# Six buffers for q and k instead of five, three for x instead of four, and spanning units scored in pairs

## The chip, the cores and the metric

The kernel runs on one core of a Trainium2 chip. The metric is the device time of one execution in microseconds (us), taken as the median of several runs. A profiled execution of the kernel gives the views that are read below.

The core has five engines that run their own instruction streams and wait for each other by semaphores. TensorE (PE in the profile, PEld for its weight loads) does matmuls. VectorE (DVE) does the search for the largest scores. ScalarE (ACT) does copies out of PSUM, exponentials and sines. GpSimd (POOL) does the folding, the splitting into halves and part of the feed-forward arithmetic. SyncE (SP) issues most of the DMAs, in order.

## The reference

Two blocks follow each other. First, attention that keeps only the 32 largest scores of each row, for 8 batches, 8 heads, 576 positions and 64 dimensions a head:

```
scores = scale * q @ k^T                       # (8, 8, 576, 576), scale = 1/8
kth    = 32nd largest of each row
scores = where(scores >= kth, scores, -1e9)
attn   = exp(scores - rowmax) / (rowsum + 1e-9)
x      = attn @ v                              # brought to (4608, 512)
```

Then a feed-forward block on the 4608 rows of x, with w_in of 512 x 2048 and w_out of 2048 x 512, in which the hidden value h is gated by its own cosine:

```
h   = x @ w_in
out = (h * cos(h)) @ w_out
```

## The kernel before

**Units and slots.** The 8 x 576 = 4608 tokens are cut into 36 tiles of 128 tokens. Each tile and each pair of heads (hp, 0 to 3) makes one unit, 144 in all, numbered 4 x tile + hp. The loop runs over 144 slots. In slot i VectorE searches the largest scores of unit i, ScalarE masks and exponentiates unit i-1, GpSimd splits unit i-2 into 16-bit halves, and SyncE writes these to DRAM (`rows`, L407) and reads them back transposed (`pT`, L413). In every even slot TensorE multiplies units i-4 and i-3 with v (`values`, L434), and VectorE scales the result into `xT` (L442).

**Spanning units.** A batch has 576 = 4.5 x 128 tokens. So the tile in the middle of each two batches holds 64 tokens of one batch and 64 of the next: tiles 4, 13, 22 and 31, units 16 to 19, 52 to 55, 88 to 91 and 124 to 127. Such a unit has two `parts` and needs q and k of both batches. In what follows 4t is the number of the first of the four units.

**Scoring.** `scores` (L226) makes the scores of a unit: columns 0 to 447 go into a PSUM tile `sc`, of which there are two, columns 448 to 575 into one of two ends of the PSUM tile `rim`, whose rest (`room`) takes the result of `values`. ScalarE copies both to SBUF in `take_scores` (L236, L237), and VectorE reads `sc` once more in `fold_high` (L245). A table `scored` says in which slot a unit is scored. A unit is scored one slot ahead (i - 1), but an even unit two slots ahead (i - 2), together with the odd unit before it: so two units are scored in an even slot and none in an odd one. Spanning units of hp 2 are an exception: `two` is false for them. Of these four units, 4t is scored in slot 4t-2 (with unit 4t-1), 4t+1 alone in slot 4t, 4t+2 alone in slot 4t+1, and 4t+3 with 4t+4 in slot 4t+2. In the profile a matmul in full precision appears as two records; a plain unit has four `sc` records and four `rim` records, a spanning one eight and eight.

**Loads.** `load_qk(b, hp)` brings q and k of a batch and a pair of heads with four DMAs on SyncE (L191 to L194), `load_v` brings v with three (L202, L207). Both take their tiles from the pool `loads`, which has five buffers for q and k each, and six for v. A load is put into the slot in which its buffer's former pair is scored for the last time (`last`), or the next slot that has no load yet (`load_at`). In the slot it comes after the slot's `rows` and `pT` on SyncE's queue.

**Feed-forward.** When the four units of a token tile are done, its feed-forward runs in pieces on TensorE between the attention's matmuls: `ff1` (L491) multiplies with w_in, ScalarE writes each piece twice, to a tile `g` (L505) and a tile `x` (L507), GpSimd reduces the argument (L527, L536), ScalarE takes the sine (L546), GpSimd multiplies `g` by it (L553), and `ff2` (L566) multiplies with w_out. `feed(n)` issues up to n pieces, on a credit that each slot adds to: 5.0, less 0.9 for each unit scored in the slot. In the last slots and after them (`ff["end"]`) VectorE takes GpSimd's part.

**Weights.** At the start the weights come in 32 chunks and are decoded by ScalarE (L133, L136), VectorE (L144) and GpSimd (L154). They are staged in the tiles of `g` (seven, `CHUNKS`) and, for every other one of the first chunks, in those of `x` (`XB`, four). The DMAs of chunks 0 to 9 are on SyncE's queue, the later ones on ScalarE's (L120).

**Order.** The order of the instructions on each engine is the one in which the program writes them down; nothing rearranges them.

Of the kernel before, what the change touches and what calls it, by code (L numbers as in the profile page):

```python
# [10 lines left out]
F32 = mybir.dt.float32  # L11
# [6 lines left out]
P = 128  # L18
# [12 lines left out]
def kernel(  # L31
# [13 lines left out]
    NT = S // P  # L45
# [7 lines left out]
    assert SCALE == 2.0 ** round(math.log2(SCALE)) and TOPK == 32 and HS <= 512  # L53

    consts = ctx.enter_context(tc.tile_pool(name="consts", bufs=1))
    loads = ctx.enter_context(tc.tile_pool(name="loads", bufs=5))
    work = ctx.enter_context(tc.tile_pool(name="work", bufs=2))
    small = ctx.enter_context(tc.tile_pool(name="small", bufs=4))
    ps = ctx.enter_context(tc.tile_pool(name="ps", bufs=2, space=bass.MemoryType.PSUM))
# [30 lines left out]
    for f in range(NF):  # L90
        w = consts.tile([P, DM], F32, tag=f"w_out{f}", name=f"w_out{f}")
        w_out.append(w)
        chunks.append((moe_w_out[f * P : (f + 1) * P, :], w))
    CHUNKS, XB = 7, 4
    BUSY = range(7, 12)
    ff = {"live": 0, "tick": 0, "now": 0, "credit": 0.0, "end": False, "kind": 0, "half": 0, "open": 0, "late": False}

# [64 lines left out]
    for t0 in range(0, B * S, P):  # L162
        parts = []
# [11 lines left out]
    for i in range(2 * NP):  # L175
        t = consts.tile([P, P], F32, tag=f"v_tail{i}", name=f"v_tail{i}")
# [21 lines left out]
    def load_v(b, hp):  # L198
        st = pairs.setdefault((b, hp), {})
        cols = slice(hp * P, (hp + 1) * P)  # L200
        t = loads.tile([P, NT, P], F32, tag="v", name="v", bufs=6)
        nc.sync.dma_start(out=t, in_=v[b, 0:MAIN, cols].rearrange("(c p) e -> p c e", p=P))  # L202
        st["v"] = t

        t = st["v_tail"] = v_tails[b % 2 * NP + hp]
        for j in range(2):
            nc.sync.dma_start(  # L207
                out=t[j * TAIL : (j + 1) * TAIL, j * D : (j + 1) * D],
                in_=v[b, MAIN:S, hp * P + j * D : hp * P + (j + 1) * D],
            )  # L210
# [64 lines left out]
    for i in range(3):  # L275
        t = consts.tile([P, 2, 2], F32, tag=f"dens{i}", name=f"dens{i}")
# [4 lines left out]
    for i in range(3):  # L281
        t = consts.tile([P, 2, TOPK + 1, 2], F32, tag=f"top{i}", name=f"top{i}")
# [345 lines left out]

    scored, last, last_values = {}, {}, {}
    for i, u in enumerate(units):  # L630
        two = i % 2 == 0 and 2 < i and (len(u["parts"]) == 1 or u["hp"] == 0)
        scored.setdefault(i - 2 if two else i - 1, []).append(u)
        for part in u["parts"]:
            last[part[0], u["hp"]] = i - 2 if two else i - 1
            last_values[part[0], u["hp"]] = i
    at_slot, at_once = {}, {}

    def load_at(i, *what):
        while i in at_slot:
            i += 1  # L640
        at_slot[i] = what

    order = [(b, hp) for b in range(B) for hp in range(NP)]
    for n in range(NP, len(order)):
        i = last[order[n - 5]] if n >= 5 else 0
        load_at(max(i, 2 * NP + 2), load_qk, *order[n])
        i = last_values[order[n - 6]] if n >= 6 else 0
        load_at(max(i + 4 - i % 2, 2 * NP + 2), load_v, *order[n])

    for hp in range(NP):  # L650
        at_once[hp] = [(load_v, 0, hp)]
# [110 lines left out]
    for i in range(NU):  # L762
# [3 lines left out]
        u, w, x = (units[i - n] if n <= i else None for n in range(3))  # L766
# [46 lines left out]
```

## Time and profile before

| | |
|---|---|
| median of three runs | 1452.13 us (1447.84 to 1453.05) |
| profiled execution | 1448.69 us, its span 1446.9 us |
| mean granted TensorE clock | 0.975 |
| busy: PE, DVE, POOL, ACT | 95%, 94%, 81%, 75% of the span |
| two ordinary slots | 18.69 us |
| DMA issue to landing, median: q, k, k, k (small) | 3.8, 3.6, 3.7, 3.3 us |

The profile's span is the time from the first to the last instruction. A line of a group names the source line, the engine, the operation, what is written and read, the count, the busy time with the mean of one, and the idle time of the engine ahead of it with what ended it. A line in order of time gives the start, the duration, the engine, the line, the operation and how many records were merged; in brackets it has the idle time of the engine ahead of it and who ended it.

### The profile page before, as it was taken

The numbers are of one execution on the slowest core, as the hardware profiler recorded it, in microseconds if no ns is written. First come the engines' busy times: TensorE is split into PE (matmuls) and PEld (weight loads), VectorE is DVE, ScalarE is ACT, GpSimd is POOL, SyncE is SP. The second block draws the span as 40 slices with busy tenths as digits, with TensorE's granted clock in tenths as the row PEclk, the third lists the DMA queues.
The fourth block names the chain that finished last, engine by engine and source line by source line (L and its number), as shares of the span: only waits on it lengthen the run. The fifth ranks groups of instructions, "written<-read, shape, count | busy, mean of one in ns | idle before, by whom it ended". The sixth has DMA issues, their size and how long they took to land.

```text
span 1446.9 us, 30176 instructions
## 1 busy us (share of the span) xinstructions
PE 1380.3 (95%) x10252; PEld 992.2 (69%) x10252; DVE 1359.4 (94%) x5237; ACT 1082.6 (75%) x1894; POOL 1166.0 (81%) x816
## 2 busy tenths in 40 slices
PE   4388899999999999999999999999999999999998
PEld 2175667777777767777777777777777776777775
DVE  7999999999999999999999999999999999999931
ACT  5787767877777777777777777777877777777742
POOL 5867888888888887888888887888888888888820
PEclk6589999999999999999999999999999999999999
DMA  8987677656665575657765566656666566655540
GB/s 257 287 230 199 175 184 180 160 158 196 174 166 140 160 190 170 170 150 187 183 166 153 145 177 177 177 151 160 197 186 150 140 170 186 156 150 153 149 104 15
DMA packets 438380, 245.25 MB, mean 170 GB/s; under 512 B 386384, under 2 KB 403025, under 8 KB 438225
## 3 DMA queue, kind: packets, MB, share of 16 engines
q1 hardware_dynamic: 429648, 222.13, 58.3%
q10 hardware_dynamic: 8576, 21.19, 4.5%
q8 instruction: 81, 1.33, 0.4%
q14 instruction: 75, 0.61, 0.1%
HBM read 45.09 MB, written 103.81 MB: 103 GB/s over the span
## 4 chain that ended last, share of the span: by engine, by line
PE 87%; DVE 7%; ACT 3%; DMA 2%; SPq 1%; POOL 0%; issue 0%; ACTq 0%
PE mm L491 33%; PE o L566 33%; PE rim L434 11%; PE sc L226 8%; DVE top L337 3%; PE rim L226 2%; DVE rest L342 2%; DMA v<-in_v_dram 1%; DMA st<-in_moe_w_in_dram 1%; DVE rest L245 1%; ACT s L366 0%; ACT s L374 0%; DVE low L342 0%; DVE w_out L144 0%; DMA k<-in_k_dram 0%
## 5 line engine op out<-in xcount | busy, mean ns | idle before, releaser
L491 PEld LDWEIGHTS mm<-xT,w_in 128*128 128x128 f32 x4608 | 536.9, 192 | 75.9 <-issue 65.2
L491 PE MATMUL mm<-xT,w_in 128*128 128x128 f32 x4608 | 539.2, 275 | 7.6 <-ACT x L507 4.8
L566 PE MATMUL o<-w_out,g 128*128 128x512 f32 x1152 | 539.7, 602 | 6.3 <-POOL w_out L154 3.7
L337 DVE MAX8 top<-rest 128x8 f32<-128x288 f32 x1152 | 478.9, 451 | 0.0
L397 POOL COPY halves<-s 128x2304 uint16<-128x2304 uint16 x144 | 303.2, 2105 | 156.4 <-ACT s L374 153.3
L342 DVE MATCH_REPLACE8 rest<-top,rest 128x288 f32<-128x288 f32 x864 | 376.5, 443 | 0.0
L566 PEld LDWEIGHTS o<-w_out,g 128*128 128x128 f32 x1152 | 202.8, 191 | 193.9 <-issue 185.3
L337 DVE MAX8 top<-low 128x8 f32<-128x288 f32 x576 | 243.6, 449 | 0.1
L374 ACT ACTIVATE s<-s,nd 128x576 f32<-128x576 f32 x288 | 220.3, 767 | 0.8
L366 ACT ACTIVATE s<-s,top 128x576 f32<-128x576 f32 x288 | 206.1, 765 | 0.0
L270 POOL TENSOR_TENSOR low<-low,rest 128x576 int32<-128x576 int32 x139 | 196.5, 1414 | 10.9
L261 POOL TENSOR_TENSOR low<-s 128x576 int32<-128x576 int32 x139 | 196.4, 1413 | 4.4 <-ACT s L237 4.4
L226 PE MATMUL sc<-k,q 64*128 64x448 f32 (+1 forms) x640 | 155.5, 587 | 37.3 <-DMA k<-in_k_dram 15.6
L505 ACT ACTIVATE g<-mm 128x512 f32<-128x512 f32 x144 | 85.9, 596 | 134.5 <-PE mm L491 130.4
L536 POOL TENSOR_TENSOR x<-g,x 128x1024 f32<-128x1024 f32 x68 | 161.0, 2367 | 5.7
L434 PE MATMUL rim<-pT,v 128*64 128x128 f32 (+1 forms) x2560 | 159.7, 269 | 5.3 <-DMA pT<-rows 5.3
L553 POOL TENSOR_TENSOR g<-g,x 128x1024 f32<-128x1024 f32 x68 | 161.0, 2368 | 0.0
L434 PEld LDWEIGHTS rim<-pT,v 128*64 128x64 f32 x2560 | 133.1, 139 | 16.1 <-issue 4.3
L236 ACT COPY s<-sc 128x896 f32<-128x896 f32 x144 | 129.3, 898 | 3.4 <-PE sc L226 2.9
L342 DVE MATCH_REPLACE8 low<-top,low 128x288 f32<-128x288 f32 x288 | 125.4, 444 | 0.0
L237 ACT COPY s<-rim 128x256 f32<-128x256 f32 x144 | 55.1, 383 | 91.8 <-PE rim L434 91.8
L226 PEld LDWEIGHTS sc<-k,q 64*128 64x128 f32 (+1 forms) x640 | 47.2, 182 | 99.9 <-DVE rest L342 47.0
(47 smaller groups left out, 1307.4 us busy)
## 6 DMA issues: line engine op xcount, KB each, us to landing
rows<-halves SPq DMA_DIRECT2D x144, 640.0 KB, 3.0
out_dram<-ob ACTq DMA_DIRECT2D x36, 256.0 KB, 2.3
q<-in_q_dram SPq DMA_DIRECT2D x31, 288.0 KB, 3.8
v<-in_v_dram SPq DMA_DIRECT2D x32, 256.0 KB, 3.5
st<-in_moe_w_out_dram ACTq DMA_DIRECT2D x16, 512.0 KB, 6.0
st<-in_moe_w_in_dram SPq DMA_DIRECT2D x10, 512.0 KB, 6.9
k<-in_k_dram SPq DMA_DIRECT2D x31, 144.0 KB, 3.6
k<-in_k_dram SPq DMA_DIRECT2D x32, 128.0 KB, 3.7
```

What stands on the lines that cost most here:

```text
L226: nc.tensor.matmul(to[r0 : r0 + rows, j, 0 : k1 - k0], st["q"][d, q0 : q0 + rows], st["k"][d, k0:k1], start=True, stop=True,)
L261: nc.gpsimd.tensor_tensor(out=u["low"].bitcast(I32), in0=s[:, :, 0:HS], in1=s[:, :, HS:S], op=ALU.add)
L270: nc.gpsimd.tensor_tensor(out=low, in0=low, in1=u["rest"][:, :, HS:S].bitcast(I32), op=ALU.subtract)
L337: nc.vector.max(to[:, j], src[:, j])
L342: nc.vector.match_replace(rest[:, j], to[:, j], src[:, j], NEG)
L366: nc.scalar.activation(out=s[:, j], in_=s[:, j], func=AF.Prelu, bias=less[:, j, 1:2], scale=1.0, alpha=FAR)
L374: nc.scalar.activation(out=s[:, j], in_=s[:, j], func=AF.Exp, bias=nd[:, j : j + 1], scale=SCALE, accum_out=den[:, j, 0:1],)
L397: nc.gpsimd.tensor_copy(out=halves[:, :, 0 : 2 * S], in_=s.rearrange("p (k h) -> p h k", h=2))
L434: nc.tensor.matmul(o[d, to], lhsT, rhs, start=c == 0, stop=c == NT)
L491: nc.tensor.matmul(mm[:, at : at + w], w_in[f // FC][:, c, (f % FC) * P : (f % FC + 1) * P], blk["xT"][:, c], start=c == 0, stop=c == NC - 1,)
L536: nc.gpsimd.tensor_tensor(out=x, in0=g, in1=x, op=ALU.subtract)
L566: nc.tensor.matmul(o, g[:, at : at + P], w_out[f], start=f == 0, stop=f == NF - 1)
```

## The change

Three things change. The pool of q and k has six buffers (v keeps six), and a load is put into the slot of the last scoring of the pair six before it instead of five. The tile `x` has three buffers instead of four, which also sets how many weight chunks are staged there. And `two` holds for every even unit after the second, so that in each of the four places unit 4t+2 is scored in slot 4t together with 4t+1, and slot 4t+1 scores nothing. A q and a k buffer together are 4,608 bytes in each partition, an x buffer 4,096.

```diff
-    loads = ctx.enter_context(tc.tile_pool(name="loads", bufs=5))
+    loads = ctx.enter_context(tc.tile_pool(name="loads", bufs=6))
...
-    CHUNKS, XB = 7, 4
+    CHUNKS, XB = 7, 3
...
-        t = loads.tile([P, NT, P], F32, tag="v", name="v", bufs=6)
+        t = loads.tile([P, NT, P], F32, tag="v", name="v")
...
-        two = i % 2 == 0 and 2 < i and (len(u["parts"]) == 1 or u["hp"] == 0)
+        two = i % 2 == 0 and 2 < i
         scored.setdefault(i - 2 if two else i - 1, []).append(u)
...
     for n in range(NP, len(order)):
-        i = last[order[n - 5]] if n >= 5 else 0
+        i = last[order[n - 6]] if n >= 6 else 0
         load_at(max(i, 2 * NP + 2), load_qk, *order[n])
```

## The prediction

> **What bounds the kernel now.** I read the page first for the busy shares and the chain of work that ended last, then the busy time by stretch, then the order of time on TensorE, then the waits.
>
> ```profile
> span 1446.9 us, 30176 instructions
> ...
> PE 1380.3 (95%) x10252; PEld 992.2 (69%) x10252; DVE 1359.4 (94%) x5237; ACT 1082.6 (75%) x1894; POOL 1166.0 (81%) x816
> ...
> PE 87%; DVE 7%; ACT 3%; DMA 2%; SPq 1%; POOL 0%; issue 0%; ACTq 0%
> ```
>
> The chain is TensorE for 87% of the span, VectorE for 7%. Next come stretches that run from the first values matmul (L434) of an even slot to that of a later one. The columns are length, then busy time and instruction count of PE, PEld, DVE, ACT and POOL, then clock, DMA share and GB/s.
>
> ```profile
> 426.05:463.43 37.38, 37.38 (x274) 27.12 (x272) 36.96 (x146) 29.28 (x52) 32.22 (x23) 1.00 0.54 149
> 482.13:500.98 18.85, 18.85 (x147) 13.47 (x145) 18.64 (x75) 15.04 (x28) 16.27 (x12) 1.00 0.54 154
> 159.45:201.43 41.98, 40.72 (x300) 27.69 (x296) 41.98 (x163) 32.35 (x58) 38.16 (x27) 1.00 0.72 190
> 500.98:539.60 38.62, 38.62 (x301) 26.87 (x297) 38.26 (x150) 29.93 (x54) 34.49 (x24) 1.00 0.70 190
> 839.14:879.02 39.88, 39.46 (x300) 27.61 (x296) 39.51 (x155) 30.27 (x54) 35.75 (x25) 1.00 0.68 184
> 1178.57:1217.04 38.47, 38.47 (x300) 26.94 (x296) 38.10 (x149) 29.78 (x54) 34.37 (x24) 1.00 0.68 190
> ```
>
> The first line is four ordinary slots: 37.38 us, TensorE without a gap, VectorE busy for 36.96. So TensorE sets the pace and VectorE has 0.42 us to spare per four slots. The second line is two slots in which one spanning unit and one plain unit are scored: 18.85 against 18.69, so a spanning unit costs TensorE 0.15 us more. The last four lines are the four places where batches meet inside a token tile (slots 16 to 19, 52 to 55, 88 to 91, 124 to 127), each as it stands on TensorE's queue. They are 1.1 to 4.6 us longer than ordinary.
>
> Where that time goes shows on TensorE in the third place:
>
> ```profile
> 866.36 1.16 PE L226 MATMUL sc<-k,q 64*64 64x448 f32 x8
> 867.16 0.58 PE L226 MATMUL rim<-k,q 64*64 64x128 f32 x8
> 867.67 1.98 PE L566 MATMUL o<-w_out,g 128*128 128x512 f32 x4
> ...
> 874.87 0.97 PE L226 MATMUL sc<-k,q 64*64 64x448 f32 x4
> 876.26 1.06 PE L226 MATMUL sc<-k,q 64*64 64x448 f32 x3 [0.42 <-DMA k<-in_k_dram]
> 876.77 0.64 PE L226 MATMUL rim<-k,q 64*64 64x128 f32 x6
> 877.16 0.54 PE L226 MATMUL sc<-k,q 64*64 64x448 f32 x1
> 877.54 0.38 PE L226 MATMUL rim<-k,q 64*64 64x128 f32 x2
> 877.85 1.02 PE L226 MATMUL sc<-k,q 64*128 64x448 f32 x4
> ```
>
> One spanning unit takes 1.13 us where nothing holds it (start 1205.78 to the next form at 1206.91). Unit 90 here takes 867.67 - 866.36 = 1.31, unit 91 takes 877.85 - 874.87 = 2.98, broken into pieces. The profile names only 0.42 us of it as idle, because the ends of matmuls are modelled; the rest hides inside stretched matmuls. The loads that these units need leave SyncE's queue just before:
>
> ```profile
> 861.82 0.53 SPq L191 DMA_DIRECT2D q<-in_q_dram  x1
> ...
> 870.85 0.58 SPq L191 DMA_DIRECT2D q<-in_q_dram  x1
> ...
> 872.64 1.00 SPq L194 DMA_DIRECT2D k<-in_k_dram  x1
> ```
>
> The page's DMA issues give 3.3 to 3.8 us from issue to landing. Issued at 870.85 to 873.64, they land near 876.3, and the units at 874.87 wait. VectorE shows the echo: "DVE xT L442 <- ACT s L237" is 7.0 us in 4 waits between 157 and 1371 us, one in each of slots 18, 54, 90 and 126.
>
> **What the Trainium skill says.** "Perfetto Trace Analysis", section "Identifying the Most-Contended Engine", holds matmul busy time a poor measure and names a repeated bubble as a sign of too few buffers. Both agree here: 0.42 us of named idle stands for 2 us lost, and the bubble returns every 36 slots. "DMA: Bandwidth & Descriptors", section "Anatomy of one DMA", says that a wait sits on the issuing sequencer, never in the DMA engine. The trace agrees: the loads of one slot come out only after the transpose ahead of them on SyncE (861.73, then 861.82). "TensorE: Matmul & The Clock Gate", part 1, says that a gap above some 3.4 us halves the clock; the gaps here stay below, and the clock is 1.00 in all six stretches, so no clock is to be won.
>
> **The change, part by part.**
>
> *Six q and k buffers.* Pair n now takes the buffer of pair n-6, so each load from batch 1, pair 1 on takes the slot that its predecessor had. That moves 27 loads of four DMAs. In a meeting place of slots 4t to 4t+3, pair 2 of the new batch leaves in slot 4t-2 instead of 4t, pair 3 in 4t instead of 4t+1. Slots with a load stay the same ones, except that slot 12 gains one (and pushes three v DMAs to slot 13) and slot 125 loses one. SyncE in slot 12 is free from 147.3, after the v load, to 150.0, in slot 13 from 156.1 to 159.0; a q,k load takes 2.3 to 2.9 us of it, the v load 1.8. Cost: 0, hidden by those gaps; without them rows and transpose go up to 1 us later, and the values matmuls that use them come at least a slot after.
>
> *Two at a time.* In each of the four places one spanning unit's eight sc and eight rim records move from slot 4t+1 to slot 4t, ahead of 40 values records (L434), 32 of L491 and 8 of L566. In slot 4t+1 nothing is scored then, so ScalarE copies the next unit's scores (L236, L237, 1.27 us) ahead of the exponentials, as in other odd slots. The order on VectorE and GpSimd is unchanged; TensorE's and ScalarE's only there. The work is equal. Behind the moved scores wait values and feed-forward matmuls of slot 4t; the score waits for the load issued in slot 4t-2 (503.59 to 506.54 in the second place, needed near 518.9) and PSUM that plain even slots free in time too. Pair 3 is issued at 522.42 to 524.74 and needed near 537, over 8 us after landing. So both waits go, and nothing else in the place is late.
>
> *Sum, by stretches.* A place should take 37.38 + 3 x 0.15 = 37.83 us (three of the four units scored in it span; the first spanning unit is scored just ahead of it). The first place also keeps a TensorE wait of 1.43 us for xT at 165.48 (0.11 is the usual distance, 1.54 is seen), so 39.26. Savings: 41.98 - 39.26 = 2.72; 38.62 - 37.83 = 0.79; 39.88 - 37.83 = 2.05; 38.47 - 37.83 = 0.64. Together **6.2 us**. *Sum, by waits*, a second way: time of the late units over 1.13. First place 2.34 and 2.53, so 2.61; second 1.90, 0.77; third 1.31 and 2.98, 2.03; fourth 1.75, 0.62. Together 6.0 us. The two agree, so the lone score itself costs almost nothing; the late load is the whole effect.
>
> *Three x tiles.* An x tile lives 21.1 us (L507 of its first half at 426 to 1300 us, gate L553 ending). Three tiles turn over in 3 x 18.69 = 56.1 us, so 35 us remain; in the tail the least is 28 us. Cost 0. At the start weight chunks 9 and 11 go into g tiles instead of x tiles. Chunk 7 then waits on SyncE for chunk 1's add (L154), which ends by 18.4, and SyncE gets there at 23.7; chunk 14 waits on ScalarE's queue for chunk 6, whose add ends by 40.54, and is issued at 41.96 (its predecessor at 41.59). Cost 0 with a margin of only 1.05 us. If the adds slip, q and k loads of the start and ScalarE's issues behind them slip by the same; bound: -1 to +5 us (one batch of four adds is 5.03). I take 0.
>
> The sum is against the profiled execution, 1448.69 us with a span of 1446.9: 1442.5. It stands 3.4 us below the median of 1452.13, which I carry unchanged: **1445.9 us**, 0.43% faster.
>
> **Rivals.**
> - *The waits are larger without the profile's luck.* They differ by place from 0.62 to 2.61 us, so they depend on when a landing falls. If the 3.4 us between the profiled execution and the median lie there, the gain is 9.6: 1442.5. For: the spread of the runs is 5.2 us. Against: the start has waits for DMA as well, 15.2 us of them in TensorE's view.
> - *VectorE takes the pace.* With 0.42 us to spare per four slots it could hide half of the gain: about 3 us, 1449. Against: its work in a place is 36.95 (slots 16 to 19, 52 to 55 alike), while TensorE needs 37.83.
> - *Slower: a weight chunk holds a queue at the start.* Fewer x tiles mean older tiles to wait for. Should chunk 14 and those behind it miss their add by a whole slot, ScalarE's queue is held for 10 us twice, and VectorE's masks and TensorE's scores with it: 20 - 6 = +14, 1466. It turns the sign once the holds exceed 6 us. Against: every chunk had its add done, the tightest 1.05 us early.
> - *The change does nothing*: a load could still wait on SyncE behind a transpose. Against: two slots, some 19 us, lie between issue and use.
>
> **How the numbers follow.** The forecast and its neighbours between 3 and 8 us saved: 0.6. Larger waits: 0.27. VectorE or nothing gained: 0.07. Slower: 0.06. A measurement of this kernel can tell about 0.5%, 7.3 us, from no change. The forecast lies 1.1 us short of it, so faster gets the 0.27 and 0.19 of the 0.6: 0.46; same the other 0.41 and 0.07: 0.48; slower 0.06. The range runs from 1439.5 (9.6 us gained, and 3 us of the runs' own spread) to 1452.0 (nothing gained).
>
> **What would show it.** Right: each place takes 37.8 us, the first about 39.3; spanning scores in unbroken eights of 1.13 us, two units one after the other in slots 16, 52, 88 and 124; TensorE's wait for k after 157 us gone; the four L442 waits of 7.0 us gone or below 1 us. Wrong: sc still broken at units 18, 19, 54, 55; VectorE gapless and TensorE with gaps in those slots; or waits of L120 and L133 grown before 60 us.

## The result, and the profile after

The changed kernel takes 1440.53 us in the median of six runs (1440.07 to 1444.68); six runs of the kernel before, three of which stand in the table above, give 1452.59 us. The ratio is 0.993, with a 95% interval of 0.9907 to 0.9952: faster by 0.7%. The profiled execution took 1440.07 us, the fastest of the six, where that of before took 1448.69.

The page of the changed kernel opens as follows; the last line is the chain by engine.

```profile
span 1438.3 us, 30154 instructions
...
PE 1372.0 (95%) x10252; PEld 989.1 (69%) x10252; DVE 1359.6 (95%) x5237; ACT 1082.4 (75%) x1894; POOL 1164.8 (81%) x816
...
PE 89%; DVE 5%; ACT 2%; DMA 2%; SPq 0%; POOL 0%; issue 0%; ACTq 0%
```

TensorE is busy for 8.3 us less (1380.3 before), with the same 10252 records, and the span is 8.6 us shorter. VectorE's busy time is unchanged (1359.4). So nearly all of what went away lay inside matmuls that the profile had counted as busy.

The busy time by stretch of the changed kernel follows, over the four places where batches meet, with the same ends on TensorE's queue as in the prediction, from the first values matmul of slot 4t-2 to that of slot 4t+2 (length; then busy and count for PE, PEld, DVE, ACT, POOL; clock; DMA share; GB/s):

```profile
158.28:197.34 39.06, 37.76 (x300) 26.85 (x296) 39.05 (x152) 31.26 (x56) 34.25 (x24) 1.00 0.74 192
496.89:534.38 37.49, 37.49 (x300) 26.77 (x296) 36.96 (x145) 29.27 (x53) 32.19 (x23) 1.00 0.69 196
833.93:871.42 37.49, 37.49 (x300) 26.77 (x297) 36.95 (x145) 29.26 (x53) 32.20 (x23) 1.00 0.69 195
1170.96:1208.46 37.50, 37.50 (x300) 26.78 (x297) 36.98 (x145) 29.27 (x53) 32.20 (x23) 1.00 0.66 179
```

Before, these were 41.98, 38.62, 39.88 and 38.47 us. The differences are 2.92, 1.13, 2.39 and 0.97: **7.4 us**. The other 1.2 us of the span lie ahead of the first place: its first line starts at 158.28 instead of 159.45. Between the places nothing moved.

Inside the third place, TensorE in order of time (start, duration, line, records):

```profile
850.47 0.98 PE L226 MATMUL sc<-k,q 64*64 64x448 f32 x8
851.27 0.40 PE L226 MATMUL rim<-k,q 64*64 64x128 f32 x8
851.49 0.93 PE L226 MATMUL sc<-k,q 64*64 64x448 f32 x8
852.24 0.40 PE L226 MATMUL rim<-k,q 64*64 64x128 f32 x8
852.57 1.09 PE L434 MATMUL rim<-pT,v 128*64 128x128 f32 x16
...
860.30 3.60 PE L566 MATMUL o<-w_out,g 128*128 128x512 f32 x8
863.73 3.73 PE L491 MATMUL mm<-xT,w_in 128*128 128x128 f32 x32
...
869.12 0.98 PE L226 MATMUL sc<-k,q 64*64 64x448 f32 x8
869.92 0.40 PE L226 MATMUL rim<-k,q 64*64 64x128 f32 x8
870.25 1.02 PE L226 MATMUL sc<-k,q 64*128 64x448 f32 x4
```

Units 89 and 90 stand one behind the other, 2.10 us for both (850.47 to 852.57), and unit 91 takes 1.13 us (869.12 to 870.25). All three are unbroken. The load that unit 91 needs now leaves on SyncE at 855.70 to 858.03:

```profile
855.70 0.53 SPq L191 DMA_DIRECT2D q<-in_q_dram  x1
...
857.44 0.59 SPq L194 DMA_DIRECT2D k<-in_k_dram  x1
```

It is issued 13.4 us ahead of the unit's first matmul, where before these were 4.0 us (870.85 to 874.87).

Every wait of VectorE between 157 and 1371 us in the changed kernel (who waited for whom; total, times, longest):

```profile
DVE den L382 <- ACT s L374: 14.6, 60, 0.4
```

Before, the same question gave two lines:

```profile
DVE den L382 <- ACT s L374: 15.1, 59, 0.4
DVE xT L442 <- ACT s L237: 7.0, 4, 2.5
```

The four waits of L442 are gone. On TensorE the wait for k is gone too, and one wait of 1.3 us for xT is left, in the first place.

### The profile page after: what moved, and what is told of

The parts are those of the page before. It is cut to its first block, busy times and chain, and to the rows that moved or that the text cites. A ratio compares the mean times of both kernels' runs of the same rounds, so it can differ in the third digit from the quotient of the medians.

```text
span 1438.3 us, 30154 instructions
## 1 busy us (share of the span) xinstructions
PE 1372.0 (95%) x10252; PEld 989.1 (69%) x10252; DVE 1359.6 (95%) x5237; ACT 1082.4 (75%) x1894; POOL 1164.8 (81%) x816
## 4 chain that ended last, share of the span: by engine, by line
PE 89%; DVE 5%; ACT 2%; DMA 2%; SPq 0%; POOL 0%; issue 0%; ACTq 0%
PE mm L491 34%; PE o L566 34%; PE rim L434 11%; PE sc L226 8%; DVE top L337 2%; PE rim L226 2%; DVE rest L342 1%; DMA st<-in_moe_w_in_dram 1%; DMA v<-in_v_dram 0%; ACT s L366 0%; DVE rest L245 0%; ACT s L374 0%; DVE low L342 0%; DVE w_out L144 0%; ACT x L507 0%
## 5 line engine op out<-in xcount | busy, mean ns | idle before, releaser
L491 PEld LDWEIGHTS mm<-xT,w_in 128*128 128x128 f32 x4608 | 536.9, 192 | 75.0 <-issue 65.2
L566 PE MATMUL o<-w_out,g 128*128 128x512 f32 x1152 | 537.1, 600 | 10.0 <-POOL w_out L154 7.7
L491 PE MATMUL mm<-xT,w_in 128*128 128x128 f32 x4608 | 539.2, 275 | 6.7 <-ACT x L507 4.8
L566 PEld LDWEIGHTS o<-w_out,g 128*128 128x128 f32 x1152 | 202.7, 190 | 197.6 <-issue 185.3
L226 PE MATMUL sc<-k,q 64*128 64x448 f32 (+1 forms) x640 | 151.4, 591 | 35.7 <-DVE rest L245 13.5
L245 DVE TENSOR_TENSOR rest<-sc,s 128x576 f32<-128x576 f32 x144 | 107.7, 748 | 6.5 <-ACT s L237 6.5
```

The costliest lines, as they stand in the source:

```text
L226: nc.tensor.matmul(to[r0 : r0 + rows, j, 0 : k1 - k0], st["q"][d, q0 : q0 + rows], st["k"][d, k0:k1], start=True, stop=True,)
L491: nc.tensor.matmul(mm[:, at : at + w], w_in[f // FC][:, c, (f % FC) * P : (f % FC + 1) * P], blk["xT"][:, c], start=c == 0, stop=c == NC - 1,)
L566: nc.tensor.matmul(o, g[:, at : at + P], w_out[f], start=f == 0, stop=f == NF - 1)
```

## The experiments

Three explanations stood against each other: the late loads, which six buffers move ahead; the order on TensorE, which scoring in pairs changes; and the start, where three x tiles could help or hurt. No run has the pairs with five buffers, or six buffers with four x tiles. Every kernel was timed beside the kernel before on the same chip. In the first group that gave 54 runs of before with a median of 1449.97 us (1447.6 to 1461.4). The six runs that gave 1452.59 thus lie somewhat high for this kernel.

### Three x tiles alone

```diff
-    CHUNKS, XB = 7, 4
+    CHUNKS, XB = 7, 3
```

> The kernel before with three x tiles and nothing else. If the x tiles cost nothing (the prediction) and the shorter start of the changed kernel's profile (1.2 us) is chance: the four places stay at 38.5 to 40 us (the first near 42), time within 2 us of before, ratio 1.000. Rival, the x tiles shorten the start: about 1.2 us faster and slots 0 to 3 some 1 us shorter. Rival, the start stalls: slower by up to 5 us.

Measured: 1449.49 us, ratio 0.9989 (0.9974 to 1.0004). The places by stretch:

```profile
158.51:201.11 42.60, 41.30 (x300) 27.61 (x296) 42.60 (x165) 32.45 (x58) 38.74 (x27) 1.00 0.72 188
500.65:539.24 38.59, 38.59 (x300) 26.88 (x296) 38.22 (x149) 29.88 (x54) 34.47 (x24) 1.00 0.70 190
838.79:878.32 39.53, 39.27 (x300) 27.17 (x296) 39.16 (x153) 30.24 (x54) 35.42 (x25) 1.00 0.66 186
1177.87:1216.31 38.44, 38.44 (x300) 26.96 (x296) 38.07 (x149) 29.74 (x54) 34.32 (x24) 1.00 0.69 190
```

The places add up to 159.16 us, against 158.95 in the profile of before, and none differs by more than 0.7 us. The x tiles neither cost nor give anything that can be told. What they do give is room in each partition; whether the sixth buffers would fit without it is not shown by any run here.

### Six buffers, spanning units of hp 2 still alone

```diff
-        two = i % 2 == 0 and 2 < i
+        two = i % 2 == 0 and 2 < i and (len(u["parts"]) == 1 or u["hp"] == 0)
```

(against the changed kernel)

> Six buffers and three x tiles, but the spanning units of hp 2 still scored alone in an odd slot. If the late load is the whole cost: each place falls to 37.5 to 37.8 us as in the changed kernel, and nearly all of the gain is here, ratio 0.993 to 0.996. Rival, scoring two at a time is what saves: places stay above 38.3 us and less than half of the gain is seen. The prediction's two sums leave 0.2 us for the lone score over all four places.

Measured: 1442.17 us, ratio 0.9951 (0.994 to 0.9962).

```profile
166.44:204.30 37.86, 37.86 (x301) 26.69 (x297) 37.86 (x149) 29.83 (x55) 34.14 (x25) 1.00 0.75 194
503.84:541.70 37.86, 37.86 (x301) 26.69 (x297) 37.48 (x147) 29.16 (x53) 33.72 (x24) 1.00 0.74 194
841.24:879.10 37.86, 37.86 (x302) 26.69 (x298) 37.50 (x148) 29.16 (x53) 33.75 (x24) 1.00 0.69 193
1178.64:1216.50 37.86, 37.86 (x302) 26.69 (x298) 37.48 (x148) 29.16 (x53) 33.75 (x24) 1.00 0.66 180
```

The order of the scores on TensorE is that of the kernel before, and every load stands in the slot that it has in the changed kernel. All four places fall to the same 37.86 us, a little above the 37.5 to 37.8 expected. So the earlier loads alone, with no pair, remove the waits: 7.8 us off the median of before, of 8.8 in the changed kernel beside it. The rest is the lone score. Here are its lines, with the feed-forward around it:

```profile
866.64 1.88 PE L566 MATMUL o<-w_out,g 128*128 128x512 f32 x4
868.45 0.98 PE L226 MATMUL sc<-k,q 64*64 64x448 f32 x8
869.25 0.40 PE L226 MATMUL rim<-k,q 64*64 64x128 f32 x8
869.58 1.98 PE L566 MATMUL o<-w_out,g 128*128 128x512 f32 x4
871.40 3.73 PE L491 MATMUL mm<-xT,w_in 128*128 128x128 f32 x32
```

From the start of the first L566 group to the L491 that follows the second (at 871.40) pass 4.76 us: 1.13 for unit 90's score and 3.63 for the two groups. Unit 89's score, alone one slot earlier, takes 1.13 more: 5.89. In the changed kernel the two scores take 2.10 and the two L566 groups, now in one run, 3.43 (860.30 to 863.73): 5.53. So the lone score costs 0.36 us a place, 0.20 in the L566 groups and 0.16 in the scores, and 1.44 us in four places. The two medians, 1.0 us apart, could not tell this, but the lengths of the places repeat to 0.01 us.

### Every load one slot later

```diff
-        load_at(max(i, 2 * NP + 2), load_qk, *order[n])
+        load_at(max(i + 1, 2 * NP + 2), load_qk, *order[n])
```

(against the changed kernel)

> The changed kernel with every q and k load one slot later than its buffer allows. If lateness of the loads is the cause: pairs 2 and 3 both leave SyncE some 5 us before their first matmul, as in the kernel before, so each place grows by two waits of 0.6 to 1.5 us, to 39 to 40 us, and 5 to 10 us in all are lost again: about the time of before. Rival, the gain comes from the order on TensorE: places stay at 37.5 us and the time stays that of the changed kernel.

Measured: 1445.23 us, ratio 0.9966 (0.9954 to 0.9979).

```profile
161.79:200.70 38.91, 38.62 (x301) 27.15 (x297) 38.91 (x152) 30.95 (x56) 34.07 (x25) 1.00 0.70 177
500.24:538.35 38.11, 38.11 (x300) 27.04 (x296) 37.56 (x147) 29.89 (x54) 32.82 (x23) 1.00 0.63 177
837.90:876.19 38.29, 38.29 (x300) 26.96 (x296) 37.75 (x148) 30.07 (x54) 32.94 (x24) 1.00 0.65 176
1175.74:1214.40 38.66, 38.42 (x301) 26.96 (x297) 38.12 (x149) 30.25 (x54) 33.30 (x24) 1.00 0.64 174
```

All but the first two loads move. The places grow again, with the order on TensorE as in the changed kernel and the buffers there, by 0.6 to 1.4 us each. Together they are 153.97 us, against 150.0 in the changed kernel run beside it, so 4.0 us; the medians differ by 4.1. The 5 to 10 us and the two waits a place that were expected did not come: only unit 4t+3 waited. In each place the two slots from 4t-2 on, which hold unit 4t+2's score, take 18.65 us as in the changed kernel. SyncE in the second place:

```profile
511.69 0.58 SPq L191 DMA_DIRECT2D q<-in_q_dram  x1
...
530.54 0.57 SPq L191 DMA_DIRECT2D q<-in_q_dram  x1
```

Pair 2 leaves 6.1 us ahead of its unit's first matmul (517.81) and is in time. Pair 3 leaves at 530.54, 4.9 us ahead of its unit's first matmul (535.43), and is not. A load of four DMAs takes 2.4 us to issue (530.54 to 532.92) and some 3.5 us to land, 5.9 together. The boundary is no sharp one: over the four places of this profile and of the three with five buffers, every load at 4.5 us or less was late and every one at 5.7 or more in time, while between them it went either way. In the third place of the three x tiles alone, pair 2 at 4.6 us (861.39 to 866.00) cost no wait; in the second place of the kernel before, run again below, pair 2 at 5.45 us (523.35 to 528.80) cost 0.25.

### The changed kernel again

No edit.

> The changed kernel once more, beside the three others on one chip. Places 37.5 us, ratio to before 0.990 to 0.996. If the 1.2 us that its first profile gained at the start is chance, the start of slot 14's values moves by as much again here, either way.

Measured: 1441.14 us, ratio 0.9941 (0.9922 to 0.9959).

```profile
160.78:198.28 37.50, 37.50 (x301) 26.77 (x297) 37.50 (x146) 29.82 (x54) 32.77 (x23) 1.00 0.75 192
497.82:535.32 37.50, 37.50 (x301) 26.78 (x297) 36.96 (x145) 29.27 (x53) 32.22 (x23) 1.00 0.72 196
834.86:872.36 37.50, 37.50 (x301) 26.78 (x297) 36.95 (x145) 29.27 (x53) 32.21 (x23) 1.00 0.69 194
1171.90:1209.39 37.49, 37.49 (x300) 26.77 (x296) 36.96 (x145) 29.26 (x52) 32.21 (x23) 1.00 0.68 179
```

The first place lacks the wait for xT here, and its values start 2.5 us later than in the first profile (160.78 against 158.28). So the 1.2 us that the first profile gained at the start are within what the start varies by. A late start doesn't by itself take the wait away: in the next experiment the values start at 160.95 us and the wait is there (39.05 us for the place).

### q and k of the first batch ahead of v

```diff
-        at_once[hp - 2].append((load_qk, 0, hp))
+        at_once[hp - 2].insert(0, (load_qk, 0, hp))
```

(against the changed kernel)

> The changed kernel with q and k of pairs 2 and 3 of the first batch ahead of v in slots 0 and 1. If what is left to gain lies in the start: TensorE's waits for k in the first 30 us shrink by some 2.5 us each, and up to 2 us are gained on the changed kernel (VectorE stands idle for 0.3 to 2 us in slots 0 to 4 of the profiles so far), ratio to before 0.992. Rival, the start waits for bytes and not for their order: same time as the changed kernel, ratio 0.994, places 37.5 us.

Measured: 1441.63 us, ratio 0.994 (0.9928 to 0.9953), the same as the changed kernel's 0.9941. TensorE's waits for k in the first 30 us are 6.9 us, where the changed kernel's two profiles have 13.5 and 6.2, so they did not clearly shrink; VectorE stood idle for 2.5 us in slots 0 to 4, against 0.3 and 1.2. The time is what the rival said; what bounds the first slots in this order was not followed further. No version beat the changed kernel.

### The kernel before again

No edit.

> The kernel before once more. Ratio 1.000 with an interval that shows what such a comparison can tell. Places: the waits fall differently from profile to profile, so 38.4 to 40 us each and the first 41 to 43; the values of slot 14 start anywhere from 158 to 167 us. If the waits were instead fixed by the program, each place would repeat its own length (38.6, 39.9, 38.5) within 0.1 us.

Measured: 1448.53 us, ratio 0.9987 (0.9976 to 0.9998). The program is the same, so a ratio within about 0.2% of one tells nothing here, whatever its interval. That of the three x tiles alone lies there too.

```profile
160.07:202.04 41.97, 40.66 (x300) 27.67 (x297) 41.96 (x163) 32.37 (x58) 38.12 (x27) 1.00 0.72 190
501.58:541.19 39.61, 39.61 (x300) 27.49 (x296) 39.24 (x153) 30.27 (x54) 35.47 (x25) 1.00 0.69 186
840.74:880.19 39.45, 39.31 (x300) 27.05 (x296) 39.08 (x153) 30.26 (x54) 35.30 (x25) 1.00 0.67 186
1179.74:1218.46 38.72, 38.72 (x300) 26.87 (x296) 38.36 (x150) 30.03 (x54) 34.57 (x24) 1.00 0.70 189
```

With five buffers the four places add up to 158.95, 159.16 and 159.75 us in three profiles, while a single place moves by up to 1 us (38.62, 38.59, 39.61 for the second). The waits are not fixed by the program, as expected, and their sum hardly changes.

## Why the prediction was right or wrong

**The bound and the waits: right.** TensorE sets the pace, the lost time hid in stretched matmuls, and it came from loads that leave too late. Six buffers alone took it away and a slot of delay brought part of it back. The named idle time of 0.42 us would have missed it; the distances from start to start did not. The signs named for being right came, but for the length of a place: scores in unbroken eights, the two units in a row, and no wait for k or of L442.

**The length of a place: the step that was mis-sized.** The prediction added 0.15 us for each of three spanning units to 37.38 and got 37.83. Measured is 37.50. The 0.15 was read from two slots with one spanning and one plain unit. It goes with the mixed pair, not with the spanning unit: two spanning units in a row take 2.10 us, two plain ones before took 2.15 (442.59 to 444.74), one of each 2.30 (869.12 to 871.42). So a place costs 0.12 us above ordinary instead of 0.45. Over four places the gain is 1.2 us larger than the 6.2 predicted.

**"The lone score itself costs almost nothing": wrong by the same amount.** The two sums, 6.2 and 6.0, agreed, and the agreement was read as proof. Neither saw that two scores in a row take less than twice 1.13 us, nor what breaking the feed-forward stream costs. With six buffers and the lone score a place took 37.86 us, so the 37.83 that was predicted for the pair is by chance the length without it. The difference, 0.36 us a place, is the same one as in the paragraph above, seen from the other side.

**What was costed at nothing.** Three x tiles alone changed the median by 0.5 us, and the interval of the ratio holds one. The load in slot 12 has no run of its own, and the profiles can't price it: the values of slot 14 start at 159.45 and 160.07 us in two profiles of before, at 158.28 and 160.78 in two of the changed kernel, and at 166.44 in that of six buffers with lone scores, whose program is the changed kernel's up to there. In this last profile TensorE waited 9.3 us for pT between 60 and 115 us, against 2.7 and 3.4, ahead of any load that moved. Its execution took 1448.13 us, 6 us above its kernel's median. ScalarE's wait for weights (L133) did not grow: 8.6 us in the changed kernel's first profile against 11.5. The margin of its queue held there: the four adds end at 39.55 us, and chunks 13 and 14 are issued from 40.23 on.

**The wait for xT in the first place.** It was to stay, and it did in the first profile (39.06 against 39.26 predicted), but in the second it was absent. What decides this was not followed.

**The time: right in range, with a part of it luck.** Predicted was 1445.9 us, measured 1440.53, 5.4 us less. Of these, 1.2 are the places, and 1.2 are the start of the first profile, which was chance. The other 3.0 are the 3.4 us between profile and median that the prediction carried unchanged: for the changed kernel they were 0.5. The range reached down to 1439.5 because it allowed for larger waits, and these did not come; the saving of 12.1 us, or 8.8 by the larger sample, lies above the 3 to 8 us that the prediction held likeliest.

The larger sample (1449.97 to 1441.14) gives the better size of the effect. The places give 7.4 us in the first two profiles, and 9.3 between the mean of three profiles of before (159.29) and the changed kernel's second (150.0); the first place's wait for xT, present in one and absent in the other, makes most of the difference. So the places hold the effect, within what the start leaves uncertain. The extra 3 us of the first comparison were not located; 54 further runs of before lie 2.6 us lower, so that sample probably fell high.

**The rivals.** The larger waits fell: three profiles of before put the sum of the places within 0.8 us. VectorE did not take the pace: outside the first place its work stayed 36.96 us, below TensorE's 37.49. Three x tiles alone did not slow the start, so the weight chunks held no queue long enough to show. The prediction had given nearly even chances to a difference above 0.5% and to a smaller one; 0.7% is above.

## What to carry to other kernels

A load that is tied to the release of its buffer can be late even when the queue and the DMA engines have time to spare: compare the time from its issue to its first use with the issue and landing times, and give it one buffer more where the time is short. When the engine that sets the pace shows no idle time, measure its steps from start to start against a stretch that is known to be undisturbed. And when two estimates agree, ask whether they share a term: here both left out what it costs to put a score alone into a stream of other matmuls.

## What the runs showed of the hardware

Two scores of the same form in a row are cheaper than one of each: 2.10 or 2.15 us against 2.30. Putting one score of 1.13 us into a run of L566 matmuls makes those take 3.63 instead of 3.43 us. A load of four DMAs whose issue began 5.7 us or more ahead of its unit's first matmul was in time, one at 4.5 us or less was late, and between these the same distance could do either. And the start of a run is by far its most variable part: in three profiles whose programs are the same up to there, the values of slot 14 start at 158.28, 160.78 and 166.44 us, while from the end of the first place to the end of the span the changed kernel took 1240.96, 1240.92 and, with q and k first, 1240.9 us.
